# Late softmax division in batch 0 and batch 1's key preparation moved behind batch 0, in a fused attention and two-mixer kernel

## The chip, the cores and the metric

The kernel runs on one core of one Trainium2 chip. The metric is the device time of one execution in microseconds, as the median of several runs. The core's engines each work through a queue of their own in order: TensorE (PE, with its weight loads shown as PEld), VectorE (DVE), ScalarE (ACT), GpSimd (POOL), and SyncE (SP), which issues the transfers.

## The reference

Three stages follow each other. Attention has 2 batches, 8 heads, 768 positions and 64 values per head. Each query sees the keys less than 16 positions away and 24 summary keys (the maximum over each block of 32 keys) with 24 summary values (the block means):

```python
k_sum = k.reshape(B, H, nb, block, D).max(axis=3)
v_sum = v.reshape(B, H, nb, block, D).mean(axis=3)
...
scores_all = np.concatenate([scores_l_m, scores_s], axis=-1)
scores_all = scores_all - np.max(scores_all, axis=-1, keepdims=True)
a = np.exp(scores_all)
a = a / (np.sum(a, axis=-1, keepdims=True) + 1e-09)
v_all = np.concatenate([v, v_sum], axis=2)
return np.matmul(a, v_all).astype(np.float32)
```

The result x (2 x 768 x 512) goes through a channel mixer with token shift (`xk = mu_k * x + (1 - mu_k) * x_prev`, then `relu(xk @ w_k)**2 @ w_v`, multiplied by the sigmoid of `xr @ w_r`), and that through a token mixer and a second channel mixer.

## The kernel before

Attention is worked in units. In batch 0 a unit is one tile of 128 queries and one half e of the head pairs (4 heads), 12 units in all. In batch 1 a unit is a tile with both halves, 6 units. A unit has four stages. `s_stage` multiplies queries and keys on PE into a PSUM tile `sp`, adds the mask and takes the minimum on DVE (line 321, tile `pe`), and takes the exponential on ACT (line 323), which also gives the row sums `den`. `n_stage` adds 1e-9 to the sums and takes the reciprocal on DVE (lines 331 and 332) and multiplies each of the unit's 4 tiles by it on POOL (line 334). `t_stage` transposes the 4 tiles on PE into a PSUM tile `pt` (line 340) and copies them to `PT`, on DVE in batch 0 (line 345) and on ACT in batch 1 (line 343). `v_stage` multiplies `PT` with the values on PE (line 360, tile `pv`), and behind the second half ACT copies the result to `xT` (line 367). `LAGS` gives the number of units by which each stage follows its `s_stage` in batch 0. PSUM has 2 tiles under the tag "pt", 2 under "s" and one under "pv"; `PEB` sets 16 `pe` tiles.

Beside attention runs `main`, the first channel mixer over 6 chunks of 256 positions. `mixed` shifts and mixes a chunk (lines 442 to 445, tiles `xk`, `xh`, `xl`); then come the products `ko` with w_k and `acc` with w_v, all of them `mm3`, line 453, three matmuls for each product of split numbers. A chunk can start when its two attention tiles are in `xT`. Each `yield` of `attention` gives a credit, multiplied by 1.2 or, from the 25th on, by 1.8, and `main` is written out until the credit is used up. Every third `yield` also converts one weight block: ACT (146), DVE (150, 156), ACT (158), POOL (159), through two buffers `wf`. `spin` puts idle matmuls into PE's queue.

Batch 1 needs key maxima (`k_max`, DVE, line 230), value sums (`vt_sum`, DVE, line 252), the spreading of the maxima into the key tiles (`kw_sums`, POOL, line 236) and the transposed value sums (`v_gather`, PE, line 259, tile `vp`, a "pt" slot). `prep_next` writes these between the units of batch 0. The order within each engine's queue is made by a scheduler from the order of the code and its priorities. Numbers behind a tile's name tell instances apart.

Of the kernel before, what the change touches and what calls it, by code (L numbers as in the profile page):

```python
# [20 lines left out]
EDGE = WINDOW - 1  # L21
BIG = 1.0e9
KB = 7
LAGS = 1, 2, 3
PEB, PTB, VB = 16, 3, 5
MW = 256
RATIO, NR, RATIO2 = 1.2, 25, 1.8
# [3 lines left out]
SPIN, SPIN_UNITS = 1, 8  # L31
WFIRST = 2
S2COST, S3COST, S4COST = 4, 5, 4
PT_ACT = (1,)
GB = 4
PIN3, PIN4 = 3, 3
PINL = True
# [15 lines left out]
def fused_kernel(ctx, tc, q, k, v, vt, mu, w_k, w_v, w_r, w_t1, w_t2, w_c1, w_c2, out):  # L53
# [22 lines left out]
    def bank(tag, bufs, shape, name):  # L76
        return ps.tile(shape, F32, tag=tag, bufs=bufs, name=name)
# [121 lines left out]
    def ahead(n):  # L199

        def wrap(fn):
            def run(*args, **kw):
                with tc.high_priority(n) if n else ExitStack():
                    return fn(*args, **kw)
            return run
        return wrap
# [2 lines left out]

    def st_of(b):  # L210
        if b not in state:
            state[b] = {"kw": {}, "qT": {}, "vw": {}, "pv": {}}
            state[b]["ks"] = at.tile([128, NP, NB], F32, tag="ks", bufs=2, name="ks")
        return state[b]

# [5 lines left out]
        kw = st_of(b)["kw"][t] = at.tile([128, NP, WC], F32, tag="kw", bufs=KB, name="kw")  # L221
        after(nc.sync.dma_start(kw[:, :, K0:K0 + 2 * HALF], k[b, t]))

    @ahead(HK)
    def k_max(b, t):

        st = state[b]
        keys = st["kw"][t][:, :, K0 + PAD:K0 + PAD + 128].rearrange("p a (n w) -> p a n w", w=BLOCK)
        n = 128 // BLOCK
        nc.vector.tensor_reduce(st["ks"][:, :, n * t:n * t + n], keys, AX.X, ALU.max)  # L230

    @ahead(HK)
    def kw_sums(b, t):
        st = state[b]
        for o in (0, WC - NB):
            nc.gpsimd.tensor_scalar(st["kw"][t][:, :, o:o + NB], st["ks"], 1.0, 1.0, ALU.mult, ALU.mult)
# [10 lines left out]
    @ahead(HR)  # L247
    def vt_sum(b, j):
        st = state[b]
        if j == 0:  # L250
            st["vr"] = at.tile([128, NP, NB], F32, tag="vrs", bufs=1, name="vrs")
        nc.vector.tensor_reduce(st["vr"][:, 2 * j:2 * j + 2], st.pop(("vt", j)), AX.X, ALU.add)

    @ahead(HR)
    def v_gather(b):
        st = state[b]
        vp = bank("pt", 2, [128, NP, 128], "vp")
        for p in range(NP):
            nc.tensor.transpose(vp[:NB, p], st["vr"][:, p], ident)
        st["vs"] = at.tile([NB, DM], F32, tag="vs", bufs=1, name="vs")  # L260
        nc.scalar.activation(st["vs"], vp[:NB].rearrange("p g e -> p (g e)"), AF.Copy, scale=1.0 / BLOCK)
# [34 lines left out]
    @ahead(HS)  # L296
    def s_stage(b, t, es):
        st = state[b]
        mask = masks[1 if t == 0 else 2 if t == NT - 1 else 0]
        kw, qT = st["kw"][t], st["qT"][t]  # L300
        sps = [bank("s", 2, [128, NP, NC], "sp") for _ in es]
        line.clear()
        for p in range(NP):
            for half in range(2):
                c0 = half * (WC - NC)
                for sp, e in zip(sps[::-1], es[::-1]):
                    r = slice(64 * e, 64 * e + 64)
                    m = nc.tensor.matmul(sp[64 * half:64 * half + 64, p], qT[r, p, 64 * half:64 * half + 64],  # L308
                                         kw[r, p, c0:c0 + NC], start=True, stop=True)
                    if len(es) > 1:  # L310
                        in_line(m)
        if PINL:
            mark.append(m)
        zs = []
        for sp, e in zip(sps, es):
            mn = at.tile([128, NP], F32, tag="mn", bufs=4, name="mn")
            den = at.tile([128, NP], F32, tag="den", bufs=4, name="den")
            P = []
            for p in range(NP):
                pe = at.tile([128, NC], F32, tag="pe", bufs=PEB, name="pe")  # L320
                nc.vector.tensor_tensor_reduce(out=pe, in0=sp[:, p], in1=mask, op0=ALU.add, op1=ALU.min,  # L321
                                               scale=-1.0 / math.sqrt(D), scalar=3.0e38, accum_out=mn[:, p:p + 1])
                nc.scalar.activation(pe, pe, AF.Exp, bias=mn[:, p:p + 1], scale=-1.0, accum_out=den[:, p:p + 1])  # L323
                P.append(pe)
            zs.append({"u": (b, t, e), "P": P, "den": den})
        return zs
# [9 lines left out]
    @ahead(HT)  # L336
    def t_stage(z):
        pt = bank("pt", 2, [128, NP, 128], "pt")
        for p in range(NP):
            nc.tensor.transpose(pt[:NC, p], z["P"][p], ident)  # L340
        z["PT"] = at.tile([NC, NP, 128], F32, tag="PT", bufs=PTB, name="PT")
        if z["u"][0] in PT_ACT:
            nc.scalar.copy(z["PT"], pt[:NC])
        else:
            nc.vector.tensor_copy(z["PT"], pt[:NC])

    @ahead(HV)
    def v_stage(zs):
        b, t, _ = zs[0]["u"]
        st = state[b]  # L350
        if t not in st["pv"]:
            st["pv"][t] = bank("pv", 1, [128, NP, 128], "pv")
        pv = st["pv"][t]
        line.clear()
        for p in range(NP):
            for half in range(2):
                for z in zs[::-1]:
                    e = z["u"][2]
                    h = 2 * p + e
                    m = nc.tensor.matmul(pv[64 * e:64 * e + 64, p, 64 * half:64 * half + 64],  # L360
                                         st["vw"][t][half][0][:, h * D:(h + 1) * D],
                                         z["PT"][:, p, 64 * half:64 * half + 64], start=True, stop=True)
                    if len(zs) > 1:
                        in_line(m)
        if zs[-1]["u"][2] == 1:
            c0 = b * XB + 1 + 128 * t
            nc.scalar.copy(xT[:, :, c0:c0 + 128], pv)

    done_tiles = [0]

    def attention():
        slots = {}
        n0 = 2 * NT
        steps = [(0, t, (e,)) for t in range(NT) for e in range(2)] + [(b, t, (0, 1)) for b in range(1, B) for t in range(NT)]
        for i in range(len(steps) + 1):
            if i < len(steps):
                b, t, es = steps[i]
                zs = s_stage(b, t, es)
                if len(es) == 1:
                    for what, z, lag in zip((n_stage, t_stage, v_stage), (zs[0], zs[0], zs), LAGS):  # L380
                        slots.setdefault(min(i + lag, n0), []).append(((i + lag, lag), what, z))
                else:
                    slots[i + 1] = [((i, 1), n_stage, z) for z in zs] + [((i, 2), t_stage, z) for z in zs] + [((i, 3), v_stage, zs)]
                if i < SPIN_UNITS:
                    spin(SPIN)
                yield 0.95 * len(es)
                if es[-1] == 1 and t + 1 < NT:
                    kw_sums(b, t + 1)
                if t == 0 and es[-1] == 1 - b * (len(es) == 1):
                    if b == 0:  # L390
                        v_gather(b)
                    vw_sums(b, 0)
            for _, what, z in sorted(slots.get(i, ()), key=lambda s: s[0]):
                what(z)
                if what is t_stage:
                    yield 0.43
                elif what is v_stage:
                    yield 0.7 * len(z)
                    done_tiles[0] += len(z) / 2
            if i < len(steps):  # L400
                if 0 in es:
                    if t + 1 < NT and t + 1 not in state[b]["vw"]:
                        vw_load(b, t + 1)
                    if b and t + 2 < NT:
                        q_load(b, t + 2)
                if 1 in es and t + 1 < NT:
                    vw_sums(b, t + 1)
                if b + 1 < B:
                    for e in es:
                        prep_next(b + 1, 2 * t + e)  # L410

    def prep_next(b, j):

        if j >= 4 and j % 2 == 0:
            k_load(b, j // 2 - 2)
        if j >= 6 and j % 2 == 0:
            k_max(b, j // 2 - 3)
        if j == 9:
            vt_load(b, 0)
            q_load(b, 0)  # L420
        if j == 10:
            vt_sum(b, 0)
            vt_load(b, 1)
        if j == 2 * NT - 1:
            for t in (4, 5):
                k_load(b, t)
            for t in (3, 4, 5):
                k_max(b, t)
            vw_load(b, 0)
            kw_sums(b, 0)  # L430
            q_load(b, 1)
            vt_sum(b, 1)
            v_gather(b)

    def mixed(t0, mu, om):
        x0 = t0 // S * XB + 1 + t0 % S
# [134 lines left out]
            nc.gpsimd.tensor_scalar(mc[64 * half:64 * half + 64], m[64 * half:64 * half + 64], 1.0, 1.0, ALU.mult, ALU.mult)  # L571
        masks.append(mc)
    for t in range(NT):
        k_max(0, t)
    kw_sums(0, 0)
    for j in range(2):
        vt_sum(0, j)
# [264 lines left out]
```

## Time and profile before

| what | value |
|---|---|
| median of 3 runs | 519.04 us (518.58 to 519.21) |
| the profiled execution: time | 519.46 us |
| the profiled execution: span | 517.4 us |
| PE busy | 491.9 us (95%) |
| DVE, ACT, POOL busy | 254.8, 203.7, 198.3 us |

The span runs from the first to the last instruction; some 2 us of the execution's time lie around it. Times inside the profile count from the start of the span. The granted clock is that of PE, as a share of full speed (2.4 GHz; half of it is 1.2 GHz).

### The profile page before, as it was taken

To read this page: it belongs to the slowest core of one execution; us is meant where nothing else is said; L and a number is where in the kernel's file an instruction comes from. 1 tells how busy PE (TensorE), PEld (TensorE's weight loads), DVE (VectorE), ACT (ScalarE), POOL (GpSimd) and SP (SyncE) were. 2 spreads that over 40 slices of the span, in tenths; PEclk is the share of its full clock that TensorE was granted. 3 is DMA by queue.
4 is the path that set the end of the run, shared out by engine and by line. 5 is a ranking of instruction groups with operands and counts; after the bars stand their busy time and mean duration, and the time that the engine had idled before them with its cause. 6 is when DMAs were issued, how large, how long until landed. Compare 5 with 4: busy or idle time off the path is not lost.

```text
span 517.4 us, 7849 instructions
## 1 busy us (share of the span) xinstructions
PE 491.9 (95%) x2968; PEld 398.9 (77%) x2968; DVE 254.8 (49%) x556; ACT 203.7 (39%) x471; POOL 198.3 (38%) x298
## 2 busy tenths in 40 slices
PE   7899687999999999999999999999999999999995
PEld 3457565888888988888867888888888888888884
DVE  3878998733335477587657766343231211311112
ACT  0668445764545645436345344344211110101100
POOL 5587887862655465378423323423100000000000
PEclk9999889899999999999999999999999999999998
DMA  8999941112005700000166351000020000200002
GB/s 269 285 286 353 326 111 33 46 53 84 7 15 209 280 1 1 1 0 2 46 239 236 133 200 42 0 2 0 1 81 1 0 0 1 81 1 0 1 0 81
DMA packets 24196, 45.39 MB, mean 88 GB/s; under 512 B 2112, under 2 KB 11328, under 8 KB 24160
## 3 DMA queue, kind: packets, MB, share of 16 engines
q1 hardware_dynamic: 24160, 44.90, 27.4%
q8 instruction: 23, 0.38, 0.3%
q14 instruction: 13, 0.11, 0.1%
HBM read 41.16 MB, written 3.15 MB: 86 GB/s over the span
## 4 chain that ended last, share of the span: by engine, by line
PE 72%; DVE 10%; DMA 5%; POOL 4%; issue 4%; SPq 2%; ACT 2%; DVEq 0%; POOLq 0%; ACTq 0%
PE o L767 19%; PE go L453 19%; PE ko L453 10%; PE acc L453 9%; PE ro L453 4%; DMA ybuf<-in_v_dram 3%; PE ho L453 3%; PE h L453 2%; PE sp L308 2%; DVE xk L443 2%; DMA wst<-in_moe_w_k_dram 2%; DVE wf L150 2%; PE pv L360 2%; PE pt L340 1%; POOL kl L468 1%
## 5 line engine op out<-in xcount | busy, mean ns | idle before, releaser
L453 PE MATMUL go<-u,w 128*128 128x512 f32 x432 | 106.7, 393 | 0.0
L159 POOL TENSOR_TENSOR w<-wf,w 128x512 fp32r<-128x512 f32 x50 | 66.7, 1337 | 82.4 <-ACT w L158 80.9
L453 PEld LDWEIGHTS go<-u,w 128*128 128x128 f32 x432 | 80.7, 188 | 17.5
L767 PE MATMUL o<-w,gh 128*128 128x512 f32 x288 | 89.0, 395 | 0.0
L682 DVE SCALAR_TENSOR_TENSOR gl<-go,gh 128x512 fp32r<-128x512 f32 x36 | 24.9, 691 | 121.1 <-ACT gh L681 121.0
L453 PE MATMUL ko<-xh,w 128*128 128x256 f32 x384 | 80.5, 295 | 0.0
L681 ACT ACTIVATE gh<-go 128x512 fp32r<-128x512 f32 x36 | 21.6, 599 | 128.7 <-PE go L453 128.7
L453 PEld LDWEIGHTS ko<-xh,w 128*128 128x128 f32 x384 | 64.4, 196 | 2.8 <-issue 0.8
L767 PEld LDWEIGHTS o<-w,gh 128*128 128x128 f32 x288 | 53.9, 188 | 12.1
L453 PE MATMUL acc<-w,kh 128*128 128x512 f32 x192 | 60.1, 400 | 0.6 <-ACT kh L467 0.6
L453 PE MATMUL ko<-xl,w 128*128 128x256 f32 x192 | 56.1, 292 | 2.2 <-DVE xl L445 2.2
L767 PE MATMUL o<-w,gl 128*128 128x512 f32 x144 | 55.4, 394 | 0.0
L158 ACT CAST w<-wf 128x512 fp32r<-128x512 f32 x50 | 31.0, 619 | 54.5 <-DVE wf L156 52.4
L156 DVE SCALAR_TENSOR_TENSOR wf<-wst,wf 128x512 int32<-128x512 int32 x50 | 43.0, 865 | 8.8 <-ACT wst L146 7.0
L323 ACT ACTIVATE pe<-pe,mn 128x120 f32<-128x120 f32 x96 | 36.7, 384 | 25.4 <-DVE mn L321 24.4
L468 POOL TENSOR_TENSOR kl<-rl,kh 128x512 fp32r<-128x512 f32 x24 | 33.1, 1381 | 32.6 <-ACT kh L467 30.9
L442 POOL TENSOR_SCALAR tmp<-xT,oms 128x256 f32<-128x256 f32 x52 | 33.9, 660 | 27.8 <-DVE xk L443 24.6
L334 POOL TENSOR_SCALAR pe<-pe,den 128x120 f32<-128x120 f32 x96 | 39.6, 432 | 12.3 <-DVE den L332 7.1
L443 DVE SCALAR_TENSOR_TENSOR xk<-xT,mus,tmp 128x256 f32<-128x256 f32 x52 | 35.4, 710 | 13.6 <-POOL tmp L442 13.5
L453 PEld LDWEIGHTS acc<-w,kh 128*128 128x128 f32 x192 | 34.4, 188 | 8.0 <-ACT kh L467 1.0
L453 PEld LDWEIGHTS ko<-xl,w 128*128 128x128 f32 x192 | 37.7, 196 | 3.6 <-DVE xl L445 2.4
L453 PE MATMUL acc<-w,kl 128*128 128x512 f32 x96 | 37.3, 404 | 0.5 <-POOL kl L468 0.5
(79 smaller groups left out, 688.6 us busy)
## 6 DMA issues: line engine op xcount, KB each, us to landing
wst<-in_moe_w_ch_dram SPq DMA_DIRECT2D x24, 512.0 KB, 4.8
wst<-in_moe_w_k_dram SPq DMA_DIRECT2D x8, 512.0 KB, 9.6
wst<-in_moe_w_v_dram SPq DMA_DIRECT2D x8, 512.0 KB, 7.1
kw<-in_k_dram SPq DMA_DIRECT2D x12, 320.0 KB, 4.1
wst<-in_moe_w_tok_dram SPq DMA_DIRECT2D x6, 512.0 KB, 7.5
out_dram<-o SPq DMA_DIRECT2D x12, 256.0 KB, 2.1
ybuf<-in_v_dram SPq DMA_DIRECT2D x12, 192.0 KB, 10.9
vw<-in_v_dram SPq DMA_DIRECT2D x12, 192.0 KB, 2.5
```

Of the source, the lines that this page charges most:

```text
L156: nc.vector.scalar_tensor_tensor(wi, top, 3, wi, ALU.logical_shift_left, ALU.bitwise_or)
L158: self.rounded.append(nc.scalar.copy(hi, wf))
L159: nc.gpsimd.tensor_tensor(lo, wf, hi.bitcast(F32), ALU.subtract)
L323: nc.scalar.activation(pe, pe, AF.Exp, bias=mn[:, p:p + 1], scale=-1.0, accum_out=den[:, p:p + 1])
L334: nc.gpsimd.tensor_scalar(z["P"][p], z["P"][p], den[:, p:p + 1], 1.0, ALU.mult, ALU.mult)
L442: nc.gpsimd.tensor_scalar(tmp, xT[:, d, x0 - 1:x0 - 1 + MW], om[:, d:d + 1], 1.0, ALU.mult, ALU.mult)
L443: nc.vector.scalar_tensor_tensor(xk[:, d], xT[:, d, x0:x0 + MW], mu[:, d:d + 1], tmp, ALU.mult, ALU.add)
L453: nc.tensor.matmul(o, l, r, start=(first and i == 0), stop=(last and i == 3 * n - 1))
L468: nc.gpsimd.tensor_tensor(lo, rl, hi.bitcast(F32), ALU.subtract)
L681: nc.scalar.activation(hi, o, AF.Relu)
L682: nc.vector.scalar_tensor_tensor(lo, o, 0.0, hi.bitcast(F32), ALU.max, ALU.subtract)
L767: nc.tensor.matmul(acc[t], l, r, start=(f == 0 and i == 0), stop=(f == nf - 1 and i == 2))
```

## The change

In batch 0 (`LATE`) the tiles are no longer multiplied before the transposes. The row sums of both halves of a tile go into one tile `dens`. Behind the tile's second value product DVE adds 1e-9 and takes the reciprocal, PE spreads the reciprocals over 128 partitions by 8 matmuls with the identity into a "pt" slot `rb`, ACT copies `pv` to `xT` as before, and DVE multiplies `xT` by `rb`. The transposes and value products follow one unit sooner. Half of batch 0's `PT` copies go to ACT. Batch 1 keeps its division. Its key maxima, value sums and their spreading are written behind all of batch 0's units, with 8 yields of together 6.0 credits between them.

```diff
-LAGS = 1, 2, 3
+LAGS = 1, 2
+LATE = (0,)
+HOLD = 6.0
...
-PT_ACT = (1,)
+PT_ACT = ((0, 0), (1, 0), (1, 1))
...
-            den = at.tile([128, NP], F32, tag="den", bufs=4, name="den")
+            if b not in LATE:
+                den = at.tile([128, NP], F32, tag="den", bufs=4, name="den")
+            else:
+                if e == 0:
+                    st["den"][t] = at.tile([128, 2, NP], F32, tag="dens", bufs=3, name="dens")
+                den = st["den"][t][:, e]
...
-        if z["u"][0] in PT_ACT:
+        if z["u"][::2] in PT_ACT:
             nc.scalar.copy(z["PT"], pt[:NC])
         else:
             nc.vector.tensor_copy(z["PT"], pt[:NC])
...
-            nc.scalar.copy(xT[:, :, c0:c0 + 128], pv)
+            if b not in LATE:
+                nc.scalar.copy(xT[:, :, c0:c0 + 128], pv)
+            else:
+                den = st["den"].pop(t)
+                nc.vector.tensor_scalar(den, den, 1e-9, None, ALU.add)
+                nc.vector.reciprocal(den, den)
+                rb = bank("pt", 2, [128, NP, 128], "rb")
+                for p in range(NP):
+                    for e in range(2):
+                        nc.tensor.matmul(rb[64 * e:64 * e + 64, p], den[:, e, p:p + 1].to_broadcast([128, D]), ident,
+                                         start=True, stop=True)
+                x = xT[:, :, c0:c0 + 128]
+                nc.scalar.copy(x, pv)
+                nc.vector.tensor_tensor(x, x, rb, ALU.mult)
...
+                if b and t == 0:
+                    yield from prep(b)
                 zs = s_stage(b, t, es)
                 if len(es) == 1:
-                    for what, z, lag in zip((n_stage, t_stage, v_stage), (zs[0], zs[0], zs), LAGS):
+                    for what, z, lag in zip((t_stage, v_stage), (zs[0], zs), LAGS):
...
-        if j >= 6 and j % 2 == 0:
-            k_max(b, j // 2 - 3)
...
-            vt_sum(b, 0)
...
-            for t in (3, 4, 5):
-                k_max(b, t)
...
-            kw_sums(b, 0)
...
-            vt_sum(b, 1)
-            v_gather(b)
+
+    def prep(b):
+
+        for t in range(NT):
+            k_max(b, t)
+            yield HOLD / (NT + 2)
+        for j in range(2):
+            vt_sum(b, j)
+            yield HOLD / (NT + 2)
+        kw_sums(b, 0)
+        v_gather(b)
```

On POOL, in the first units of batch 0 of the kernel before, the queue holds the multiplications of line 334 (`pe` by `den`), the copies of the value sums and the first weight blocks (`w`):

```order
L334 TENSOR_SCALAR pe_284<-pe_284,den_274 128x120
L286 COPY ybuf_71<-vs_296 24x512 x5
L334 TENSOR_SCALAR pe_319<-pe_319,den_318 128x120
L334 TENSOR_SCALAR pe_322<-pe_322,den_318 128x120
L334 TENSOR_SCALAR pe_325<-pe_325,den_318 128x120
L334 TENSOR_SCALAR pe_328<-pe_328,den_318 128x120
L159 TENSOR_TENSOR w_500<-wf_496,w_500 128x512
```

At the same place of the changed kernel:

```order
L287 COPY ybuf_71<-vs_295 24x512 x5
L161 TENSOR_TENSOR w_477<-wf_473,w_477 128x512
L161 TENSOR_TENSOR w_541<-wf_537,w_541 128x512
L161 TENSOR_TENSOR w_565<-wf_561,w_565 128x512
L466 TENSOR_SCALAR tmp_547<-xT_84,oms_67 128x256
L466 TENSOR_SCALAR tmp_550<-xT_84,oms_67 128x256
```

All 48 multiplications of batch 0 are gone, and the weight blocks follow each other directly.

On PE, where `main` begins (the first `ko`), the kernel before has all of tile 4's value products (`pv_1037`) behind it, and only the last two units' transposes and tile 5's products to come:

```order
L340 MATMUL pt_1002<-ident_61,pe_794 120x128
L360 MATMUL pv_1037<-PT_918,ybuf_71 64x64 x8
L340 MATMUL pt_1002<-ident_61,pe_797 120x128
L360 MATMUL pv_1037<-PT_1007,ybuf_71 64x64 x8
L453 MATMUL ko_611<-xh_588,w_500 128x256
L453 MATMUL ko_611<-xl_589,w_500 128x256
```

In the changed kernel it begins behind tile 3's products (`pv_782`) and their spreading (`rb_874`); `pt_851` takes the "pt" slot that `rb_705` held:

```order
L309 MATMUL sp_1001<-kw_109,xT_84 64x120 x8
L346 MATMUL pt_851<-ident_61,pe_738 120x128
L346 MATMUL pt_851<-ident_61,pe_741 120x128
L346 MATMUL pt_851<-ident_61,pe_744 120x128
L346 MATMUL pt_851<-ident_61,pe_747 120x128
L366 MATMUL pv_782<-PT_777,ybuf_71 64x64 x8
L382 MATMUL rb_874<-ident_61,dens_522 64x128 x8
L477 MATMUL ko_568<-xh_545,w_477 128x256
L346 MATMUL pt_945<-ident_61,pe_806 120x128
L346 MATMUL pt_945<-ident_61,pe_809 120x128
L346 MATMUL pt_945<-ident_61,pe_812 120x128
L346 MATMUL pt_945<-ident_61,pe_815 120x128
```

The value products of tiles 4 and 5, two more spreadings and one `spin` now stand among the first `ko` products.

On DVE, ahead of batch 1's first unit, the kernel before works through weight blocks and a chunk's mixing before the first score tile (`pe_1108`):

```order
L150 TENSOR_SCALAR wf_1016<-wst_157 128x512
L156 SCALAR_TENSOR_TENSOR wf_1016<-wst_157,wf_1016 128x512
L443 SCALAR_TENSOR_TENSOR xk_1505<-xT_84,mus_66,tmp_1508 128x256
L443 SCALAR_TENSOR_TENSOR xk_1505<-xT_84,mus_66,tmp_1511 128x256
L321 ISA pe_1108,mn_1106<-sp_1088,mask1_183 128x120
L321 ISA mn_1106 128x1
```

In the changed kernel the first score tile is `pe_1250`, behind tile 5's multiplication (line 386):

```order
L253 TENSOR_REDUCE vrs_1205<-ybuf_71 128x48
L158 SCALAR_TENSOR_TENSOR wf_932<-wst_153,wf_932 128x512
L152 TENSOR_SCALAR wf_955<-wst_155 128x512
L158 SCALAR_TENSOR_TENSOR wf_955<-wst_155,wf_955 128x512
L386 TENSOR_TENSOR xT_84<-xT_84,rb_1350 128x4x128
L327 ISA pe_1250,mn_1248<-sp_1230,mask1_183 128x120
L327 ISA mn_1248 128x1
L152 TENSOR_SCALAR wf_962<-wst_157 128x512
```

It no longer stands behind the chunk's mixing (`xk`), and one weight block now lies between the unit's score tiles.

## Rows read from the trace of the kernel before

**Rows 1.** The page: 40 slices of the span, busy tenths of PE, granted clock.

```profile
PE   7899687999999999999999999999999999999995
...
PEclk9999889899999999999999999999999999999998
```

**Rows 2.** Busy time by stretch: length, then PE, PEld, DVE, ACT, POOL; clock; DMA.

```profile
13.60:58.30 44.70, 38.44 (x388) 26.00 (x386) 37.18 (x155) 32.16 (x118) 33.33 (x70) 1.00 1.07 312
58.30:97.50 39.20, 31.17 (x229) 26.13 (x227) 37.30 (x79) 21.24 (x53) 30.23 (x36) 0.87 0.41 111
97.50:260.00 162.50, 162.43 (x1215) 139.92 (x1214) 87.75 (x183) 84.95 (x190) 91.46 (x120) 1.00 0.17 58
260.00:300.00 40.00, 37.86 (x165) 29.58 (x164) 25.81 (x38) 17.72 (x32) 14.41 (x12) 1.00 0.58 204
300.00:508.00 208.00, 208.00 (x925) 169.87 (x924) 60.09 (x95) 46.33 (x80) 20.93 (x16) 1.00 0.07 23
```

**Rows 3.** The same columns for the three stretches at a lower granted clock.

```profile
60.90:63.70 2.80, 2.77 (x13) 2.78 (x14) 2.80 (x5) 1.22 (x2) 1.48 (x3) 0.50 1.12 277
67.60:70.60 3.00, 3.00 (x15) 2.93 (x16) 3.00 (x6) 0.98 (x3) 2.03 (x5) 0.50 0.76 179
90.10:94.60 4.50, 4.12 (x38) 3.59 (x39) 4.50 (x17) 4.30 (x18) 2.27 (x3) 0.62 0.32 92
```

**Rows 4.** What PE waited for, 13.6 to 97.5: total us, times, longest.

```profile
PE pv L360 <- DVE PT L345: 4.2, 4, 1.4
PE sp L308 <- issue: 3.6, 2, 3.1
PE vp L259 <- DVE vrs L252: 3.2, 3, 2.4
PE ko L453 <- DVE xl L445: 2.2, 1, 2.2
```

**Rows 5.** Timeline of PE, one half's value products in batch 0: start, us.

```profile
45.52 1.15 PE L360 MATMUL pv<-PT,ybuf 120*64 120x64 f32 x16
46.59 0.65 PE L340 MATMUL pt<-ident,pe 128*120 128x128 f32 x4
```

**Rows 6.** Timeline of PE, both halves' value products in batch 1.

```profile
105.95 1.15 PE L360 MATMUL pv<-PT,vw 120*64 120x64 f32 x32
107.03 0.65 PE L340 MATMUL pt<-ident,pe 128*120 128x128 f32 x4
```

**Rows 7.** Timeline of PE, one spin and what follows it.

```profile
29.88 1.13 PE L532 MATMUL spin<-ident 128*128 128x512 f32 x2
30.93 0.82 PE L308 MATMUL sp<-kw,xT 64*64 64x120 f32 x10
```

**Rows 8.** DVE's groups, 13.6 to 97.5: busy us, mean ns, idle before.

```profile
L345 DVE COPY PT<-pt 120x512 f32<-120x512 f32 x12 | 8.1, 677 | 0.0
...
L331 DVE TENSOR_SCALAR den<-den 128x4 f32<-128x4 f32 x15 | 5.5, 368 | 0.6 <-ACT pe L323 0.5
...
L332 DVE RECIPROCAL den<-den 128x4 f32<-128x4 f32 x14 | 2.4, 168 | 0.1
```

**Rows 9.** POOL's two costliest groups, 13.6 to 97.5.

```profile
L334 POOL TENSOR_SCALAR pe<-pe,den 128x120 f32<-128x120 f32 x51 | 21.1, 431 | 5.3 <-DVE den L332 2.3 <-ACT xT L367 1.8 <-PE pt L340 1.2
L159 POOL TENSOR_TENSOR w<-wf,w 128x512 fp32r<-128x512 f32 x15 | 20.9, 1402 | 3.2 <-ACT w L158 3.0
```

**Rows 10.** DVE adding PSUM to SBUF, 128x512, 280 to 320.

```profile
L712 DVE TENSOR_TENSOR ybuf<-ho,ybuf 128x512 f32<-128x512 f32 x12 | 7.9, 681 | 2.0 <-PE ho L453 2.0
```

**Rows 11.** ACT's copy of transposes in batch 1: ns min/median/max.

```profile
L343 ACT COPY PT<-pt x12: 567/588/594, 100.9 to 165.0; 120x512 f32<-120x512 f32 x12
```

**Rows 12.** ACT's copy of the value products: ns min/median/max.

```profile
L367 ACT COPY xT<-pv x12: 565/587/592, 33.6 to 169.8; 128x512 f32<-128x512 f32 x12
```

**Rows 13.** What DVE waited for, 15.6 to 97.5.

```profile
DVE pe L321 <- PE pt L340: 4.6, 3, 3.4
...
DVE wf L150 <- POOL w L159: 1.5, 1, 1.5
```

**Rows 14.** Timeline of DVE ahead of batch 1's first score tiles.

```profile
87.30 1.88 DVE L443 SCALAR_TENSOR_TENSOR xk<-xT,mus,tmp 128x256 f32<-128x256 f32 x2
89.11 0.27 DVE L321 CUSTOM_DVE_ANT_0 pe<-sp,mask 128x120 f32<-128x120 f32 x1
```

More of the change, by code (lines that the diff above doesn't have):

```diff
@@ L211, in st_of @@
         if b not in state:
-            state[b] = {"kw": {}, "qT": {}, "vw": {}, "pv": {}}
+            state[b] = {"kw": {}, "qT": {}, "vw": {}, "pv": {}, "den": {}}
             state[b]["ks"] = at.tile([128, NP, NB], F32, tag="ks", bufs=2, name="ks")
@@ L222, in k_load @@
         after(nc.sync.dma_start(kw[:, :, K0:K0 + 2 * HALF], k[b, t]))
-    @ahead(HK)
     def k_max(b, t):
@@ L573, in fused_kernel @@
     for t in range(NT):
-        k_max(0, t)
+        ahead(HK)(k_max)(0, t)
     kw_sums(0, 0)
```

## The prediction

> **What bounds the kernel now.** I read the page first, for where PE falls short. Its slices show two weak places in the first fifth of the span, and a clock below full speed only there and at the very ends [rows 1]. From 97.5 on PE is busy without a gap except for 2.1 us between 260 and 300 [rows 2], so behind 97.5 the time is PE's amount of work, and what is won ahead of it is kept. Then I cut the start by stretches. From 13.6 to 58.3, while batch 0's attention runs alone, PE is busy 38.44 of 44.70 us: 6.3 idle. From 58.3, where `main`'s first product starts, to 97.5 it is busy 31.17 of 39.20: 8.0 idle [rows 2]. In that second stretch DVE is busy 37.30 of 39.20, so DVE sets the pace there. Three stretches run at half clock: the first two lose half of their busy 2.77 and 3.00 us, 1.4 and 1.5; the third, at a mean of 0.62 over 4.5 us, spent 0.76 of it at half speed, 3.4 us, and loses 1.7 [rows 3]. Together PE loses 6.3 + 8.0 + 4.6 = 18.9 us ahead of 97.5. This is all that there is to win at the front.
>
> The table of waits names the owners of the idle time: the value products wait 4.2 us for DVE's `PT` copies, the value sums' transposes 3.2 (2.4 of it once, in the second stretch) for DVE's sums, `main` 2.2 for `xl`, and 3.6 stand at batch 1's scores without a named releaser, 3.1 of it once [rows 4]. I read the last as a DVE wait too: batch 1's scores fill both "s" slots, and the score tiles that would free them stand on DVE behind two mixing operations that end at 89.1 [rows 14].
>
> **What the change removes.** POOL loses 48 multiplications. The window has 51 of them, 21.1 us [rows 9], so 48 are 19.9 us of the 62 to 64 that POOL is busy in the two stretches (33.33 + 30.23) [rows 2]. POOL doesn't end PE's waits by itself, but the weight blocks of line 159 (15 in the window, 1402 ns each) come sooner on it, and DVE waited 1.5 us for one of them [rows 9, 13]. DVE loses 6 of 12 pairs of add and reciprocal, at 368 and 168 ns: 3.2 us, or 2.0 if one long add, which held the mean up, is left out [rows 8]; I take 2.0. It also loses 6 `PT` copies at 677 ns, 4.1 us [rows 8]; these go to ACT at 588 ns, 3.5 us [rows 11]. ACT is busy 32.16 of the first 44.70 us [rows 2], so they fit, but its queue is in order: weight preparation and exponentials stand behind each copy, and DVE waits for the first of these.
>
> **What it adds.** DVE gets 6 multiplications of 128x512 with one operand in PSUM. The nearest row is an add of that shape with one operand in PSUM, 681 ns [rows 10], so 4.1 us. DVE's sum is 4.1 - 2.0 - 4.1 = -2.0 us.
>
> PE gets 6 times 8 matmuls that spread the reciprocals, 64 output rows and 128 columns each, alternating between the lower and upper half of the output. The trace has none, so I bound them. Each f32 matmul is recorded as two passes. In batch 0 one half's products, 16 passes of 64 columns, take 46.59 - 45.52 = 1.07 us [rows 5]; in batch 1, where the two halves alternate, 32 such passes take 107.03 - 105.95 = 1.08 us [rows 6]. So alternating halves run side by side. A spreading is 16 passes of 128 columns, as many columns as those 32 passes: 1.08 us, six of them 6.5. If they ran one after the other, the price is that of `spin`, 1024 columns in 30.93 - 29.88 = 1.05 us [rows 7]: 2.1 each, 12.6 in all. I take 6.5, since the row with alternating halves has nearly the same rows in use (120 of 128). The Trainium skill speaks against it: "TensorE: Matmul & The Clock Gate", in the mechanism of packing small matmuls, says that a weight load overlaps running matmuls only where the row group differs, and here every matmul uses all rows. By that rule the six cost 12.6. The trace disagrees for the products of 120 rows [rows 5, 6]; no run here shows 128.
>
> **What it moves.** Transposes no longer wait for the division, and follow one unit sooner. `main` begins behind tile 3's spreading and not behind tile 4's products; tiles 4 and 5's products then stand among the `ko` products and fill the 2.2 us wait for `xl`. Batch 1's six maxima, two sums and spreading keep their amount and stand later in DVE's and POOL's queues; PE's transposes of the sums stand behind 48 `ko` products instead of 24, so I take their 2.4 us as gone (bound: it stays). Batch 1's score tiles stand on DVE ahead of the mixing, with one weight block between them, so of the 3.4 us at the scores I keep 1.5. The transfers are the same in number; the first of batch 1's value transfers is issued two places sooner.
>
> **The new wait.** A spreading holds one of two "pt" slots until ACT has copied `pv` and DVE has multiplied: 1.08 + 0.587 + 0.681 = 2.35 us [rows 10, 12], against 0.65 of transposes [rows 5] and 0.677 of copy [rows 8], 1.33, for a common use. That is 1.0 us longer. PE's queue is in order: at `pt_851` the next value products, the spreading and `main`'s first product stand behind it. I count one such hold, 1.0, in the open, and take the other five as lying beside score products; the multiplication itself waits on DVE for ACT, with score tiles and weight blocks behind it.
>
> **The sum.** PE's idle time afterwards: in the first stretch, 6.3 less half of the 4.2 for `PT`, plus 1.0, 5.2; in the second, 8.0 - 2.2 - 2.4 - 1.9 = 1.5. The three slow stretches came behind waits of 2.2, 2.4 and 3.1 us; the longest that I expect is 1.5, so I keep one slow stretch, 1.5. Together 8.2. The gain is 18.9 - 8.2 - 6.5 = 4.2 us: 519.46 becomes 515.3. The profiled execution lies 0.4 above the median of the runs, 519.04, so for the median I say **514.8**.
>
> **The rivals.** (1) *Large gain.* POOL's relief reaches everything: no wait for `PT`, no hold, no slow stretch. Then 2.1 + 1.5 stay, the gain is 18.9 - 6.5 - 3.6 = 8.8: 510.2. For it speaks how much POOL loses; against it that the waits name DVE. (2) *DVE stays the bound.* DVE does 2.0 us less, but the six multiplications each may stand up to 0.59 us [rows 12] for ACT's copy, 3.5 in all. From -2.0 to +1.5, middle -0.3: 518.8, no change. For it speaks that DVE is full from 58.3 on; against it the first stretch, where DVE had waits of 4.6 us for transposes to free `pe` tiles [rows 13], which come sooner now. (3) *The hold ends on the other side.* If all six holds lie open, 6.0 us and not 1.0, waits as long as before come back ahead of `main`, and with them the two slow stretches that I dropped, 3.1: 514.8 + 5.0 + 3.1 = 522.9, slower. It decides where holds and slow stretches together cost 5.2 us more than I count, 0.9 for each spreading. For it speaks that PE's queue is in order and that batch 0 uses 18 "pt" slots where it used 12; against it that most spreadings have score products behind them that need no slot. (4) *The spreadings run one after the other.* 12.6 and not 6.5: 520.9, slower; it decides from 1.95 us each. This is the rule named above, told in rows: [rows 7] speak for it, [rows 5, 6] against.
>
> **Chances and range.** Forecast 0.62; large gain 0.10; no change 0.11; holds 0.10; spreadings 0.07. A measurement of this kernel tells 0.2%, 1.0 us, from no change. So faster 0.72, same 0.11, slower 0.17. The range takes in the large gain and the case of no change, 509.5 to 520.0, and leaves out the holds and the spreadings, 0.17. The forecast's own range is 512 to 518.
>
> **What the profile afterwards would show.** Each spreading near 1.1 us on PE (near 2.1: rival 4). The first `xl` product some 4 us ahead of 60.9, with PE then busy. PE's idle time before saturation near 7 us, and its saturation near 93.3. No line 334 in batch 0. A wait of PE's transposes for DVE's line 386 of 1 us in total; 5 or more would be rival 3. One slow stretch; three with as much idle time as before would bring rival 2. I would be wrong if ACT, with 3.5 us more, kept DVE's weight blocks waiting by more than the 4.2 us forecast.

## The result and the profile after

The changed kernel takes 512.13 us (median of 4 runs, 511.0 to 513.5); the ratio to the kernel before is 0.987, 95% interval 0.9839 to 0.9901. The median is 6.9 us lower, where 4.2 were forecast; 512.13 lies inside the range. The profiled execution took 511.19 us with a span of 509.4. The profiles of two experiments below (the key preparation alone, and the base with 5.0 credits) fell on disturbed executions, and only their times are used.

The page of the changed kernel, to be laid beside [rows 1]: PE's busy tenths, and the granted clock.

```profile
PE   7999897999999999999999999999999999999995
...
PEclk9999999999999999999999999999999999999999
```

Of the two weak places a slice of 8 and one of 7 tenths are left, and no slice has a clock below 9 tenths. The windows put numbers to it (length, then PE, PEld, DVE, ACT, POOL; clock; DMA):

```profile
13.60:51.30 37.70, 36.69 (x415) 25.97 (x412) 32.84 (x130) 31.28 (x112) 15.88 (x22) 1.00 1.06 313
51.30:90.50 39.20, 33.93 (x301) 26.79 (x300) 37.91 (x83) 22.73 (x62) 26.93 (x35) 1.00 0.60 172
90.50:97.50 7.00, 6.61 (x66) 5.10 (x66) 5.14 (x31) 6.33 (x24) 7.00 (x14) 1.00 0.00 0
260.00:300.00 40.00, 40.00 (x183) 32.68 (x182) 25.25 (x45) 19.39 (x33) 13.34 (x10) 1.00 0.50 174
```

`main`'s first product now stands at 51.3 and not at 58.3. Ahead of it PE is idle for 1.0 us (before 6.3, [rows 2]); from there to 90.5, a stretch as long as that of before, 5.3 (before 8.0). No stretch runs at half clock, where three did [rows 3], and the 2.1 us between 260 and 300 are gone. DVE is as full as before in the second stretch, 37.91 of 39.20. What PE waited for, 13.6 to 95:

```profile
PE acc L477 <- ACT kh L491: 1.9, 2, 1.0
PE ko L477 <- DVE xl L469: 1.0, 1, 1.0
PE sp L309 <- issue: 0.9, 1, 0.9
PE ko L477 <- ACT w L160: 0.6, 1, 0.6
PE vp L260 <- DVE vrs L253: 0.5, 1, 0.5
...
PE pt L346 <- DVE xT L386: 0.2, 1, 0.2
```

Every owner named in [rows 4] has shrunk: `PT` from 4.2 to nothing, the value sums from 3.2 to 0.5, the scores from 3.6 to 0.9, `xl` from 2.2 to 1.0. The longest single wait was 3.1 and is 1.0. The new wait, PE's transposes for the late multiplication, is 0.2 in all. The timeline shows a spreading (tile `rb`) behind value products, and the first `xl` product; the last row is that product in the kernel before:

```profile
42.97 0.97 PE L366 MATMUL pv<-PT,ybuf 120*64 120x64 f32 x13
43.73 0.32 PE L382 MATMUL rb<-ident,dens 128*64 128x128 f32 x1
...
43.95 1.04 PE L382 MATMUL rb<-ident,dens 128*64 128x128 f32 x14
44.92 0.33 PE L346 MATMUL pt<-ident,pe 128*120 128x128 f32 x1
...
53.20 0.39 PE L477 MATMUL ko<-xl,w 128*128 128x256 f32 x1 [1.04 <-DVE xl L469]
```

```profile
60.92 0.58 PE L453 MATMUL ko<-xl,w 128*128 128x256 f32 x1 [2.19 <-DVE xl L445]
```

From the first `rb` at 43.73 to the next work at 44.92 are 1.2 us, with three value passes among them. The last 14 of the 16 passes take 44.92 - 43.95 = 0.97, so all 16 take 1.1, as forecast. The first `xl` product comes 7.7 us earlier than at 60.92.

### The profile page after: what moved, and what is told of

Same layout as the page of the kernel before. It is cut to its first block, busy times and chain, and to the rows that moved or that the text cites. A ratio compares the mean times of both kernels' runs of the same rounds, so it can differ in the third digit from the quotient of the medians.

```text
span 509.4 us, 7950 instructions
## 1 busy us (share of the span) xinstructions
PE 492.6 (97%) x3064; PEld 399.6 (78%) x3064; DVE 249.1 (49%) x544; ACT 206.4 (41%) x477; POOL 186.4 (37%) x250
## 4 chain that ended last, share of the span: by engine, by line
PE 79%; DVE 9%; POOL 4%; issue 3%; ACT 2%; DMA 2%; SPq 1%; DVEq 0%; POOLq 0%; ACTq 0%
PE o L791 19%; PE go L477 19%; PE ko L477 10%; PE acc L477 10%; PE ro L477 5%; PE ho L477 3%; PE h L477 3%; PE sp L309 3%; PE pv L366 2%; DVE xk L467 2%; PE pt L346 2%; DMA xT<-in_vt_dram 1%; PE spin L556 1%; DVE wf L152 1%; PE utr L745 1%
## 5 line engine op out<-in xcount | busy, mean ns | idle before, releaser
L161 POOL TENSOR_TENSOR w<-wf,w 128x512 fp32r<-128x512 f32 x50 | 68.7, 1379 | 85.5 <-ACT w L160 78.8
L477 PE MATMUL ko<-xh,w 128*128 128x256 f32 x384 | 77.0, 289 | 0.7 <-ACT w L160 0.6
L477 PEld LDWEIGHTS ko<-xh,w 128*128 128x128 f32 x384 | 61.4, 188 | 4.5 <-issue 1.3
L477 PE MATMUL ko<-xl,w 128*128 128x256 f32 x192 | 54.6, 284 | 1.0 <-DVE xl L469 1.0
L492 POOL TENSOR_TENSOR kl<-rl,kh 128x512 fp32r<-128x512 f32 x24 | 34.5, 1437 | 34.6 <-ACT kh L491 31.2
L466 POOL TENSOR_SCALAR tmp<-xT,oms 128x256 f32<-128x256 f32 x52 | 38.1, 742 | 23.1 <-DVE xk L467 15.0
L158 DVE SCALAR_TENSOR_TENSOR wf<-wst,wf 128x512 int32<-128x512 int32 x50 | 41.4, 834 | 8.4 <-ACT wst L148 6.9
L490 DVE TENSOR_TENSOR rl<-rl 128x512 f32<-128x512 f32 x24 | 18.9, 785 | 46.7 <-ACT rl L489 46.3
L467 DVE SCALAR_TENSOR_TENSOR xk<-xT,mus,tmp 128x256 f32<-128x256 f32 x52 | 39.2, 784 | 4.2 <-POOL tmp L466 3.8
L477 PEld LDWEIGHTS ko<-xl,w 128*128 128x128 f32 x192 | 36.2, 189 | 2.1 <-DVE xl L469 1.3
## 6 DMA issues: line engine op xcount, KB each, us to landing
wst<-in_moe_w_ch_dram SPq DMA_DIRECT2D x24, 512.0 KB, 4.6
wst<-in_moe_w_k_dram SPq DMA_DIRECT2D x8, 512.0 KB, 7.6
wst<-in_moe_w_v_dram SPq DMA_DIRECT2D x8, 512.0 KB, 10.3
wst<-in_moe_w_tok_dram SPq DMA_DIRECT2D x6, 512.0 KB, 4.5
```

The source lines that it names most:

```text
L158: nc.vector.scalar_tensor_tensor(wi, top, 3, wi, ALU.logical_shift_left, ALU.bitwise_or)
L161: nc.gpsimd.tensor_tensor(lo, wf, hi.bitcast(F32), ALU.subtract)
L466: nc.gpsimd.tensor_scalar(tmp, xT[:, d, x0 - 1:x0 - 1 + MW], om[:, d:d + 1], 1.0, ALU.mult, ALU.mult)
L467: nc.vector.scalar_tensor_tensor(xk[:, d], xT[:, d, x0:x0 + MW], mu[:, d:d + 1], tmp, ALU.mult, ALU.add)
L477: nc.tensor.matmul(o, l, r, start=(first and i == 0), stop=(last and i == 3 * n - 1))
L490: nc.vector.tensor_tensor(rl, rl, rl, ALU.mult)
```

## The experiments

Each ratio is to the kernel before, with its 95% interval; the third column is that ratio times 519.04. Idle is PE's idle time in the profile from 13.6 to 97.5 (83.9 us less its busy time in three windows), and clock loss is the sum over the stretches below full clock of length times what is missing of the clock (without the last microseconds of the span, where the clock falls in every kernel). Most experiments have 5.0 credits; as that base has no profile here, their profiles are laid beside that of the changed kernel, with 6.0.

| kernel | ratio (interval) | us | span | idle | clock loss |
|---|---|---|---|---|---|
| before | 1 | 519.0 | 517.4 | 14.3 | 5.1 |
| changed | 0.987 (0.9839 to 0.9901) | 512.3 | 509.4 | 6.7 | 0 |
| late division only | 0.9861 (0.9837 to 0.9884) | 511.8 | 511.9 | 6.3 | 3.4 |
| key preparation only | 0.995 (0.9934 to 0.9966) | 516.4 | | | |
| base, 5.0 credits | 0.9859 (0.9834 to 0.9883) | 511.7 | | | |
| copies on DVE | 0.9928 (0.9904 to 0.9953) | 515.3 | 514.0 | 9.3 | 1.7 |
| POOL ahead | 0.9874 (0.9835 to 0.9913) | 512.5 | 509.1 | 6.7 | 0 |
| POOL behind | 0.9988 (0.9965 to 1.0012) | 518.4 | 516.0 | 10.0 | 3.4 |
| spread twice | 0.9961 (0.9944 to 0.9977) | 517.0 | 514.7 | 3.6 | 0 |
| spread by half | 0.9944 (0.9924 to 0.9964) | 516.1 | 514.8 | 6.4 | 5.1 |
| no division, 6.0 | 0.9888 (0.9866 to 0.991) | 513.2 | 512.0 | 6.8 | 5.1 |
| no division, 5.0 | 0.984 (0.9817 to 0.9863) | 510.7 | 507.4 | 6.7 | 3.4 |
| no idle matmuls | 0.9985 (0.9964 to 1.0006) | 518.3 | 516.5 | 9.7 | 15.4 |
| 4 idle matmuls | 0.9936 (0.99 to 0.9973) | 515.7 | 515.1 | 11.2 | 5.1 |

### Which part of the change makes the gain

**Late division only.** The key preparation goes back between batch 0's units:

```diff
+    @ahead(HK)
     def k_max(b, t):
...
-                if b and t == 0:
-                    yield from prep(b)
...
+        if j >= 6 and j % 2 == 0:
+            k_max(b, j // 2 - 3)
```

> This kernel has the late division, the new lags and ACT's copies, but batch 1's key preparation is written between batch 0's units as in the kernel before. Theory A: the gain is made by the late division in the first stretch (no multiplication on POOL ahead of the transposes, no wait for PT, main's first xl product 7.7 us earlier), and the moved preparation only takes away the 3.2 us of waits for the value sums. By A this kernel lies 1 to 3 us behind the changed kernel, 513 to 515.5, its first xl product stands near 53, and the waits for the value sums (before: 3.2 us) are back in the second stretch. Rival B: the moved preparation makes the gain, because DVE is full from 40 to 74 and maxima and sums stand ahead of score tiles there. By B this kernel is at 517 to 519 and its first xl product near 58 or later.

It is as fast as the changed kernel, faster than theory A allowed, so B falls and A was too timid: the waits for the value sums didn't come back (0.5 us, as in the changed kernel). The late division, with its lags and ACT's copies, takes them away without the move. The first `xl` product stands at 55.2. This kernel's profiled execution took 513.74 us, and its other three runs 511.68 to 512.22; the windows of the profile show where this one lost time:

```profile
18.60:22.10 3.50, 3.50 (x14) 1.74 (x14) 2.91 (x19) 2.35 (x13) 0.20 (x1) 0.52 1.07 336
90.10:93.80 3.70, 3.70 (x10) 2.76 (x10) 3.70 (x23) 2.24 (x10) 3.16 (x6) 0.54 0.19 63
```

These are two stretches at half clock, 3.4 us of clock loss in a run that took some 2 us more. The changed kernel's own four runs fall into the same two groups: 511.0 and 511.2 at a mean clock of 0.999 and 0.998, 513.1 and 513.5 at 0.992. By these mean clocks the same program gets such stretches in some executions and not in others; only one of the four has a profile.

**Key preparation only.** The kernel before with `prep` and its credits, the division early:

```diff
+                if b and t == 0:
+                    yield from prep(b)
...
-        if j >= 6 and j % 2 == 0:
-            k_max(b, j // 2 - 3)
```

> This kernel has the early division of the kernel before, and only batch 1's key preparation is moved behind batch 0's units, with the 6.0 credits between its steps. Theory A: the first stretch keeps its 6.3 us of idle time and its PT waits of 4.2 us, the first xl product stays near 60; what can go is the 3.2 us for the value sums and the 3.1 us at batch 1's scores, and the slow stretches behind them, so 514.5 to 518.5. Rival B: maxima and sums out of DVE's way bring most of the gain, 512 to 514, with the PT waits down to 1 us or less.

It is 2.6 us faster than before, in the middle of A's range. Alone it is worth something; on top of the late division it is worth nothing that can be measured. That the two parts take away the same waits is the likely reading; no profile of this kernel shows it.

**The base for the rest.** `HOLD` is 5.0:

> The changed kernel with 5.0 credits between the steps of batch 1's key preparation, not 6.0: the base for the next kernels, chosen since with 5.0 fewer single products of different tiles alternate on PE in all of them. In the trace of the kernel without division at 6.0, 15 groups of two pv passes alternate with single acc or ko products between 107.88 and 117.8, with a period of 0.68 us where the same work in blocks takes 0.30. If that reading is right and the credits don't matter otherwise, this kernel is within 1 us of the changed one, 511 to 513. If the credits decide (rival B), it differs by 2 us or more.

It is within 0.6 us of the changed kernel: here the credits decide nothing that can be measured. It is the base of all that follow, but for the first kernel without division and the one that spreads twice, which have 6.0.

**Copies on DVE.**

```diff
-PT_ACT = ((0, 0), (1, 0), (1, 1))
+PT_ACT = ((1, 0), (1, 1))
```

> The changed kernel (5.0 credits) with all of batch 0's PT copies on DVE, as before the change: 6 copies of 677 ns go back to DVE, which is full from 40 to 74. If DVE paces this stretch, 4.1 us come back in part: 514 to 516.5, with waits of the value products for PT. If the copies were not what mattered: 511 to 513.

It is 3.6 us slower than the base: about half of the change's gain (7.3 us by the same column) hangs on ACT's six copies, but not through waits for `PT`, of which there are still none. What PE waited for, and the windows:

```profile
PE sp L309 <- issue: 4.3, 2, 2.6
PE acc L477 <- ACT kh L491: 2.2, 1, 2.2
```

```profile
51.30:90.50 39.20, 34.31 (x345) 27.37 (x341) 37.92 (x97) 24.59 (x75) 26.56 (x39) 1.00 0.53 150
90.50:97.50 7.00, 4.45 (x24) 2.61 (x23) 6.53 (x30) 5.57 (x21) 3.84 (x6) 0.83 0.00 1
```

DVE's extra 4.1 us come out at batch 1's scores (4.3 where the changed kernel has 0.9; the unnamed releaser read as DVE's score tiles, as in [rows 14]). The longest of these waits, 2.55 us, ends at 93.5, and one stretch at half clock begins at 95.1.

**POOL ahead and POOL behind.** POOL multiplies batch 0's 48 score tiles by 1.0, ahead of the transposes or behind them:

```diff
+    @ahead(HN)
+    def side_stage(z):
+        for p in range(NP):
+            nc.gpsimd.tensor_scalar(z["P"][p], z["P"][p], 1.0, 1.0, ALU.mult, ALU.mult)
...
+                if what is t_stage and z["u"][0] in LATE:
+                    side_stage(z)
```

> The changed kernel (5.0 credits) with POOL multiplying batch 0's 48 score tiles by 1.0 in place ahead of the transposes: the 20 us of POOL's work and its place in the chain come back, the values stay. If POOL's relief and the shorter chain make the gain, it is gone: 517 to 520, with PE waiting for PT or for pe again. If the gain comes from something else (ACT's share of the copies, the lags, the spreadings as filler), it stays at 511 to 514.

> The same 48 multiplications by 1.0 on POOL, but behind the transposes, so that POOL has the load of the kernel before and no transpose waits for it. The values stay. If the load counts (weight blocks of line 161 and mixing queue behind it, DVE waits for them): as the kernel with the multiplications ahead, 516 to 520. If only the place in the chain counts: 511 to 514.

Ahead, with 15.7 us of work put back on POOL and into the chain, the kernel is as fast as the changed one. The trace of POOL ahead, 13.6 to 100:

```profile
PE pv L371 <- DVE PT L356: 1.9, 2, 1.6
PE pt L351 <- DVE PT L356: 1.1, 1, 1.1
```

```profile
57.71 0.38 PE L484 MATMUL ko<-xh,w 128*128 128x256 f32 x1
```

3.0 us of waits for `PT` are back; the two longest end at 51.65 and 55.32. Up to 51.3 PE idles for 2.7 us (1.0 in the changed kernel), from there to 90.5 for 4.0 (5.3), and behind it not at all (0.4): 6.7 in both. `main`'s first product stands at 57.71, hardly ahead of the 58.3 of the kernel before, so its earlier start in the changed kernel isn't what carries the gain. The forecast that POOL's relief itself ends no wait that matters holds. Behind the transposes the 48 multiplications cost 6.7 us, which neither theory gave for the place alone. POOL waited 10.2 us for those transposes with its queue in order, and batch 1's multiplication came late:

```profile
PE pt L351 <- POOL pe L340: 4.0, 2, 3.7
PE ko L484 <- DVE xl L476: 2.1, 1, 2.1
```

```profile
87.50:94.40 6.90, 6.16 (x23) 4.51 (x24) 4.92 (x23) 4.25 (x18) 6.90 (x10) 0.51 0.00 1
```

Line 340 is batch 1's own multiplication: PE stands 3.7 us at once for it, to 87.44, and 6.9 us at half clock begin there. So POOL's load alone is not what counts. That its queue, standing for the transposes, made line 340 late is argued and not shown: the last of those waits of POOL's ends at 47.52. Right ahead of line 340, which starts at 87.02, POOL waited for DVE twice, 0.37 us each, and the reciprocal that line 340 needs ended on DVE at 86.3.

### What the late division costs

**No division.**

```diff
-                den = st["den"].pop(t)
-                nc.vector.tensor_scalar(den, den, 1e-9, None, ALU.add)
...
-                x = xT[:, :, c0:c0 + 128]
-                nc.scalar.copy(x, pv)
-                nc.vector.tensor_tensor(x, x, rb, ALU.mult)
+                st["den"].pop(t)
+                nc.scalar.copy(xT[:, :, c0:c0 + 128], pv)
```

> Batch 0's division is left out here: no spreading, no add and reciprocal, no multiplication; batch 0's attention rows stay undivided. The difference from the changed kernel is the price of the late division. By the prediction's price: 6.5 us on PE and 1.0 for the hold of the slot, so 504.5 to 506.5. Theory A': the spreadings lie partly in time in which PE would be idle anyway, since DVE is full from 40 to 74 and sets the pace there, so taking them away gives back only part: 508 to 511, with PE idle for more than the 6.3 us of the changed kernel between 13.6 and 90.5. A third way: without the six multiplications DVE is ahead too, main starts earlier, and the gain is larger than the PE work: under 504.

With 6.5 us less work on PE it is no faster than the changed kernel, and all three expectations missed. In its timeline the `acc` products first stand alone, then alternate with batch 1's value products:

```profile
102.55 0.63 PE L468 MATMUL acc<-w,kh 128*128 128x512 f32 x2
103.01 0.40 PE L468 MATMUL acc<-w,kl 128*128 128x512 f32 x1
103.25 0.63 PE L468 MATMUL acc<-w,kh 128*128 128x512 f32 x2
...
107.88 0.33 PE L366 MATMUL pv<-PT,vw 120*64 120x64 f32 x2
108.14 0.49 PE L468 MATMUL acc<-w,kh 128*128 128x512 f32 x1
108.56 0.33 PE L366 MATMUL pv<-PT,vw 120*64 120x64 f32 x2
108.82 0.49 PE L468 MATMUL acc<-w,kh 128*128 128x512 f32 x1
```

Three `acc` products take 103.25 - 102.55 = 0.70, 0.23 each, and two value passes 0.07 in a block [rows 6], 0.30 together. Alternating they take 108.56 - 107.88 = 0.68. It goes on so for 15 rounds, by this reading 5.7 us that have nothing to do with the division. Hence the base with 5.0 credits, where the order has fewer of these, and the kernel once more:

> Batch 0's division is left out again (its rows stay undivided), with 5.0 credits, so that the value products of batch 1 don't alternate with acc products over 10 us. Theory A'': the alternation cost the first kernel without division 15 times 0.38, 5.7 us, and the true price of the late division shows here: 508 to 510, 2 to 4 us ahead of the changed kernel, less than the 6.5 of PE work, since PE then waits for DVE instead. Rival: the spreadings cost nothing, since PE idles as long as they take and its clock falls in the waits: 511.5 to 514, with two or more stretches at half clock ahead of 90. Second rival: the whole 6.5 comes back: 504.5 to 506.

It is 1.0 us ahead of the base, with intervals that overlap; between the first theory (2 to 4) and the rival (nothing). It is 2.5 us ahead of the first kernel without division, with five such rounds left and one stretch at half clock less (1.7 us), so the 5.7 us of the alternation don't come back in full. The windows:

```profile
50.60:54.30 3.70, 3.70 (x21) 3.70 (x20) 3.50 (x6) 2.68 (x8) 3.32 (x4) 0.54 1.09 342
81.50:85.00 3.50, 3.50 (x36) 2.97 (x36) 3.47 (x9) 2.98 (x13) 3.50 (x4) 0.51 0.00 0
```

Without the spreadings two stretches fall to half clock: one at 50.5, behind a wait of 2.2 us for `xl` that ends at 50.24, one at 81.5, behind a wait of 1.8 for batch 1's multiplication that ends at 79.8. They lose 3.4 of the 6.5 us that the spreadings take in the changed kernel; PE's idle time is the same 6.7. So in this profile half of the spreadings' work is paid back in clock, and the four runs point the same way (mean clocks of 0.987 to 0.991, those of the base 0.993 to 0.999). The span is 2.0 us shorter than the changed kernel's, not 3.1; 1.1 is not assigned.

**Spread twice.**

```diff
-                for p in range(NP):
+                for p in [*range(NP)] * 2:
```

> Each of the 48 spreading matmuls is issued twice, so the values stay the same and only PE's amount of work and the time that a pt slot is held grow. If a spreading is 1.08 us of PE work and PE is the bound, this kernel is slower than the changed one by 6 times 1.08, 6.5 us, less the 1.0 us that PE is idle in the first stretch: 517.5 to 519, and a spreading takes 2.1 to 2.2 us. If halves ran one after the other (2.1 for a single spreading) it would be 12.6 us, 525. If the longer hold of the pt slot starts waits for the multiplication of line 386, 2 to 6 us come on top of the 6.5: 520 to 525, with pt waits for line 386 or for ACT's copy, which the changed kernel has at 0.2 us.

It is 4.7 us slower than the changed kernel by the ratios, just under the expected range, and a pair of spreadings takes 45.52 to 47.59, 2.1 us. No wait for the late multiplication appears though the slot is held 1 us longer: the hold isn't what limits here.

**Spread by half.**

```diff
-                for p in range(NP):
-                    for e in range(2):
+                for e in range(2):
+                    for p in range(NP):
```

> The changed kernel (5.0 credits) with each spreading's 8 matmuls in another order: four into the lower half of the output, then four into the upper. Theory A (halves overlap only where they alternate): a spreading takes 2.1 us and not 1.1, PE has 6 us more work, 516.5 to 518.5. Rival: a spreading takes 1.1 in any order, since each pass costs the same 0.07 us wherever it lands: 511 to 513.

It is 4.4 us slower than the base, just under the range of theory A, but the spreading is not what that theory said. The timeline:

```profile
51.59 1.58 PE L382 MATMUL rb<-ident,dens 128*64 128x128 f32 x16
53.10 1.04 PE L309 MATMUL sp<-kw,xT 64*64 64x120 f32 x16
```

A spreading takes 1.51, between the 1.1 and the 2.1. So 6 times 0.4, 2.4 us, are the spreadings' part. The clock alone isn't the rest: runs of this kernel at a mean clock of 0.995 took 515.2 to 515.7, a run of the base at 0.996 took 511.5. Some 1.5 us stay open. Alternation helps, but half after half is not serial either.

### The idle matmuls and the clock

**No idle matmuls, and 4 of 8.**

```diff
-SPIN, SPIN_UNITS = 1, 8
+SPIN, SPIN_UNITS = 1, 0
```

> The changed kernel (5.0 credits) without the 8 idle matmul groups between batch 0's units: 8 times 1.05, 8.4 us less PE work between 13.6 and 63. If PE is the bound there since the change (it idles for 1.0 us of 37.7), the gain shows: 504 to 507. If DVE paces the stretch (it is full from 40 to 74) and the idle matmuls fill its waits, PE idles 5 us or more there instead and the time stays at 510 to 513. If the clock falls in these waits, stretches at half clock come back and it is 513 to 517.

It is slower by 6.6 us than the base, with 8.4 us less work on PE, a little past the third case. The windows show the clock's part (a third stretch at half clock, 98.2 to 101.6, follows):

```profile
16.20:36.80 20.60, 20.25 (x162) 16.03 (x161) 12.80 (x68) 15.54 (x61) 5.21 (x7) 0.50 1.09 284
53.60:60.80 7.20, 6.36 (x45) 5.73 (x46) 6.99 (x19) 5.66 (x15) 2.24 (x2) 0.53 1.10 346
```

With `SPIN_UNITS` 4, a version meant to beat both kernels:

> The changed kernel (5.0 credits) with idle matmuls behind the first 4 units of batch 0 and not behind 8: 4 times 1.05, 4.2 us less PE work, and the transposes and value products of tile 1 no longer alternate one by one (0.9 us). Without any idle matmuls the clock was at half speed from 16 to 37 and from 53.5 to 61. Theory A (the spreadings take over the work of the later idle matmuls, which only the first units still need): no stretch at half clock ahead of 37, 506.5 to 509, faster than both kernels. Rival (PE's waits grow by as much, and one or two stretches come back): 510 to 513.

It misses: 4.0 us slower than the base. The first half of theory A held, since no stretch falls ahead of 49.5, but PE's idle time is 11.2 us, where the changed kernel has 6.7, the longest wait being this one:

```profile
PE pt L346 <- DVE PT L351: 3.4, 1, 3.4
```

and 10.1 us at half clock (50.0 to 53.3 and 87.5 to 94.3) followed. No version that keeps the division beats the changed kernel by more than the intervals.

## Why the prediction was right, point by point

**The direction and the place were right.** The gain is made ahead of 97.5 and kept: the second half of both kernels is saturated.

**The sum was right by luck.** Its remaining loss, 8.2 us, measured 6.7, but its three terms were each mis-sized. For the first stretch I kept 5.2 us of idle time; it has 1.0; 3.1 of the difference are the half of the waits for `PT` that I kept and the open hold, and neither is there. For the second I kept 1.5; it has 5.3 up to 90.5 and 0.4 behind it. The waits there are for `kh` and `w` from ACT (1.9 and 0.6), for `xl` (1.0) and at the scores (0.9); that DVE, busy 37.91 of 39.20, paces them is a reading and not shown. For the slow stretches I kept 1.5; the profiled execution has none, though two of the four runs, at a clock of 0.992, seem to have had some. Two errors the one way, 4.2 and 1.5, and one the other, 4.2, left the sum near. Behind 97.5 PE idled 2.2 us before and 1.1 now, a gain that I left out. So 18.9 + 0.5 (the clock loss of before is 5.1 by finer windows, not 4.6) - 6.7 - 6.5 + 1.1 = 7.3 us of the 8.0 by which the span is shorter; 0.7 is not assigned.

**The spreadings' price** of 1.08 each stands, and rival 4 with its 2.1 falls, in the changed kernel and even half after half (1.51). The rule of the Trainium skill that spoke against it ("TensorE: Matmul & The Clock Gate", the mechanism of packing small matmuls, by which weight loads overlap only between different row groups) gives 2.1 here, if serial matmuls cost what [rows 7] say; the trace has 1.1 with all 128 rows in use. But as the price of the step it is too high: without the division the kernel gains 1.0 us and not 6.5, and in that profile the clock takes 3.4 of it back.

**The holds** (rival 3) cost 0.2 (the prediction named 1 in total), and doubling the spreadings started no such wait. They are not harmless in every order: without idle matmuls PE stands 2.8 us at once for the late multiplication. **DVE as the bound** (rival 2) is half true: DVE stays full, and giving it 4.1 us back costs 3.6. **The large gain** (rival 1) was forecast at 510.2. The profile has three of its marks (no wait for `PT`, no hold, no slow stretch), but 5.3 us of idle time in the second stretch where it kept 1.5. Its mechanism, POOL's relief, is refuted by the kernel that multiplies ahead.

**What I took for nothing and was much:** the moved copies had no term of their own beyond DVE's sum of -2.0; they decide 3.6 us. **What I took for something and was nothing:** 2.4 us for the moved value sums and 1.9 for the scores came without moving the preparation at all.

**Open:** what else, beside ACT's copies, carries the gain. The new lags, by which transposes and value products follow one unit sooner, were never run without the late division, and so stand as a rival to it. The kernel before with ACT's copies alone was not run, nor was the early division without its trip through DVE's add and reciprocal; the kernel that multiplies ahead waits for exponentials only, and points there without showing it.

This ledger (idle time, clock loss and work of PE against the span) holds between some of the kernels, too: from the changed kernel to POOL behind, idle time +3.3 and clock loss +3.4 make 6.7, the span 6.6; to copies on DVE 2.6 and 1.7 make 4.3, the span 4.6; to 4 idle matmuls 4.5 and 5.1 less 4.2 of work make 5.4, the span 5.7. It is 1.8 us off for both other spreadings (twice: 6.5 of work less 3.0 make 3.5, the span 5.3; by half: 2.4 and 5.1 less 0.3 make 7.2, the span 5.4) and 2.9 without idle matmuls (3.0 and 15.4 less 8.4 make 10.0, the span 7.1).

## To carry to other kernels

Where an in-order engine waits for another that is full, moving a small copy to a third engine can be worth more than taking four times its work off an engine that nobody waits for (4.1 us of copies against 15.7 here); see first for whom each queue stands. A cost on PE ahead of its saturation is not its busy time alone: count with it the waits it fills and the clock it holds. An experiment that takes work away may pay for it in another order of PE's queue, so compare idle time, clock loss and alternations before calling the difference a price.

## What was not expected of the hardware

Matmuls of different tiles that alternate singly can be dear: a pair of value passes (120 rows) and one `acc` product (128 rows) take 0.68 us where in blocks they take 0.30. In the changed kernel one transpose and two value passes alternate from 34.18 on, 0.51 a round, where in blocks they take 0.30 at most (a quarter of 0.65 and an eighth of 1.07, [rows 5]):

```profile
34.18 0.32 PE L346 MATMUL pt<-ident,pe 128*120 128x128 f32 x1
34.43 0.33 PE L366 MATMUL pv<-PT,ybuf 120*64 120x64 f32 x2
34.69 0.33 PE L346 MATMUL pt<-ident,pe 128*120 128x128 f32 x1
```

Not every pair is: from 109.18 on one transpose and one `ko` product alternate in the changed kernel at 0.23 a round, no dearer than in blocks (a quarter of 0.65 and 0.12).

The idle matmuls earn more than they cost: without their 8.4 us of work the kernel is 6.6 us slower. Of the 20 stretches at half clock in the profiles, 13 begin in a wait of 1.7 to 3.7 us, at its end or within 2 us behind it; four other waits of 1.8 to 2.3 us passed without one, and by the mean clocks the same program ran with such stretches and without, some 2 us apart. Once down, the clock stayed down through work: from 16.2 to 36.8, in the kernel without idle matmuls, PE was recorded busy for 20.25 of 20.60 us at 1.2 GHz.
